# Products of x with w1 and w2 in eleven block products instead of twelve, with single buffers for V, q, xT and a gate tile

## The chip, the cores and the metric

One core of a Trainium2 chip runs the whole program. The metric is the device time in microseconds. The kernel before was run three times: 569.05, 569.18 and 569.51 us.

## The reference

A linear recurrence with complex gates (4 batches, 8 heads, 768 steps, head dimension 48) gives x, and four matrix products follow on x (3072 rows of 384). Everything is fp32 on the chip.

```
# per batch and head; a = a_re + i*a_im, its magnitude cut to at most 0.999
for t in range(S):
    S_re, S_im = ar*S_re - ai*S_im + k[t] v[t]^T,  ar*S_im + ai*S_re
    y[t] = q[t] @ S_re
x = y transposed to (B*S, H*D)            # 3072 x 384
a = x @ w1 ; b = x @ w2                   # 384 x 1024 each
out = ((a * b) @ w3) @ w_out              # 1024 x 1024, 1024 x 384
```

## The kernel before

**Tiling.** The work is cut into eight units, `u` = 0 to 7: a batch and half of its 768 steps, so 384 rows of x (`TT`) in three chunks of 128 (`UC` = 3). w3 and w_out are multiplied with each other once at the start (`fuse`, L973), and `w3o`, 1024 x 384, stands for both after that.

**A unit.** `gates(u)` turns the loaded gates, q and k into decayed and rotated forms. It is a chain that alternates between ScalarE (logarithm, exponential, arctangent, sine, with two loads of a function table) and VectorE (scans at L590 and L615, products from L566 to L638). Tiles of 128x1152 pass through it: `re`, `im`, `gA`, `gZ`, and `gR` and `k`, which are its results along with `gA` and `q`. DMAs then move `gR` and `k` into `KL`, `gA` and `q` into `QL` (`move`). `turn` (L671) transposes `gR` and `k` on TensorE, and ScalarE copies the result to `KT`. `state` (L721) multiplies `KT` with V and adds to the running state `T`. `scores` (L683) multiplies `KL` with `QL`, and VectorE copies the causal part to `A` (L685, the mask). `outputs` (L710) makes y from `A`, V, `T` and `QL`, and ScalarE copies it to `xT`, chunk by chunk (L712). `spread_v` (L524) copies the loaded `vr` into the padded layout V, which two buffers hold.

**The products of a unit.** `ffn_ab(u, j)` (L744) makes one block of 128 columns of x·w1 and x·w2: two PSUM tiles `m` of 128x384, three matmuls each. ScalarE copies the first to `a` (L749), VectorE multiplies the second with it (L750) into `ab`. Eight such blocks make a unit. `out_sums`, `out_pair` (L795) and `ffn_out` (L831) then multiply `ab` with `w3o`: for units 1 to 7, two of the three row blocks go through seven products of half blocks with sums on VectorE (L770, L777), ScalarE copying the first to `U` (L800), and the third row block goes plainly.

**Order.** TensorE's order is written out by hand: `ffn(u)` is a list of parts, and `unit(u)` runs the first four parts of unit u-1 (`AHEAD`), then alternates further parts with the pieces of unit u (transposes, state, scores, outputs), so that the last y of a unit is followed by the last parts of the output products and then by the next unit's blocks. `gates(u+1)` is a generator that is stepped on beside these parts. On the other engines a scheduler sets the order, by program order, readiness in its own estimate, and `tc.high_priority()` for what empties PSUM; each engine then works through its list strictly in order. PSUM tiles `m`, `p` and `o` share four buffers (`ps_m`). In units 2 and later ScalarE also works on "looks" (`check_weights`, L918 to L921), which go over the raw weights and the gates a block at a time, with DMAs of their own on SP.

**Buffers.** The pool `one` has single buffers, `two` double ones; `gate_pool` gives even and odd units each a buffer for `q`, `k`, `gA`, `gR`. `late` holds what is needed after the weights are in.

Of the kernel before, what the change touches and what calls it, by code (L numbers as in the profile page):

```python
# [374 lines left out]
def kernel(  # L375
# [36 lines left out]
    nc = tc.nc  # L412
# [44 lines left out]

    Ab = [singles.tile([P, H, C], FP, name=f"A{i}") for i in range(2)]
    Vb = [singles.tile([P, UC, H, 64], FP, name=f"V{i}") for i in range(2)]

# [36 lines left out]
    def take_qk(u):  # L497
        g = g_t.setdefault(u, {})
        g["q"] = gate_pool[u % 2].tile([P, KD, TT], FP, tag="q", name="q")
        g["k"] = gate_pool[u % 2].tile([P, KD, TT + 1], FP, tag="k", name="k")  # L500

    def load_qkv(u):
        b, h = divmod(u, 2)
        if "q" not in g_t.get(u, {}):
            take_qk(u)
        g = g_t[u]
        load_rows(g["k"], kt, u)
        load_rows(g["q"], qt, u)
        if u:
            load_v(u)  # L510

# [8 lines left out]
    def spread_v(u):  # L520
        vr = g_t[u]["vr"].rearrange("p c (h two d) -> p c h two d", two=2, d=D)
        V = Vb[u % 2].rearrange("p c (h two) e -> p c h two e", two=2)
        for i, e0 in enumerate((0, 64 - D)):
            nc.scalar.copy(out=V[:, :, :, i, e0:e0 + D], in_=vr[:, :, :, i])  # L524

# [12 lines left out]

    masked, begun = [], []

    def gates(u, split):

        b, h = divmod(u, 2)
        g = g_t.setdefault(u, {})
        A = gate_pool[u % 2].tile([P, KD, TT], FP, tag="gA", name="gA")
        R = gate_pool[u % 2].tile([P, KD, TT + 1], FP, tag="gR", name="gR")
# [9 lines left out]
        tt, ts, stt = nc.vector.tensor_tensor, nc.vector.tensor_scalar, nc.vector.scalar_tensor_tensor  # L556

        chain(nc.scalar.preload_act_table_set("natural_log_exp_and_others"))
        for s in parts:
            act(out=A[:, s], in_=re[:, s], func=AF.Ln)  # L560
            act(out=r[:, s], in_=A[:, s], func=AF.Exp, scale=-1.0)
            if u == 1:
                tc.add_manual_dep(chained[-1].ins, fused[-1].ins.name, ORDER, reason="unit 0 first")
# [14 lines left out]
        for s in parts:  # L578
            begun[:] = [stt(out=A[:, s], in0=Z[:, s], scalar=0.5, in1=A[:, s], op0=OP.mult, op1=OP.add)]
            act(out=Z[:, s], in_=A[:, s], func=AF.Exp, scale=-1.0, bias=EPS)  # L580
            act(out=Z[:, s], in_=Z[:, s], func=AF.Copy, scale=-1.0, bias=1.0)
            act(out=A[:, s], in_=A[:, s], func=AF.Exp)
        yield

        for s in parts:
            least = ts(out=A[:, s], in0=A[:, s], scalar1=0.999, scalar2=None, op0=OP.min)
            if u == 1:
                tc.add_manual_dep(least.ins, masked[-1].ins.name, ORDER, reason="scores first")
            for f in range(s.start, s.stop):
                nc.vector.tensor_tensor_scan(out=A[:, f], data0=A[:, f], data1=Z[:, f], initial=1.0,  # L590
                                             op0=OP.mult, op1=OP.mult)
# [12 lines left out]
        for X in (R[:, :, TT], K2[:, :, TT], st_dec[:, u]):  # L604
            nc.scalar.copy(out=X, in_=A[:, :, TT - 1])
        if u:
            spread_v(u)
        yield
# [82 lines left out]
    def outputs(u, c):  # L691
        QL = L_t[u][0]
        w = slice(c * C, (c + 1) * C)
        A, V = Ab[(u * UC + c) % 2], Vb[u % 2][:, c]
        if c == 0:
            xT_t[u] = two.tile([P, KD, TT], FP, tag="xT", name="xT")
        T = T_t.get((u // 2, u % 2 * UC + c))
        first = T is None
        y = ps_v.tile([P, KD, C], FP, tag="v", name="y")
        lanes = [[] for _ in range(4)]  # L700
        for i, q in enumerate(QUADS):
            f, j = divmod(i, 4)
            o = y[32 * j:32 * j + 32, f]
            got = [(V[:, hd, 32 * e:32 * e + 32], A[:, hd]) for hd, e in q]
            if not first:
                got += [(T[:, hd, 32 * e:32 * e + 32], QL[:, hd, w]) for hd, e in q]
            lanes[j] += [(o, a, b, n == 0, n == len(got) - 1) for n, (a, b) in enumerate(got)]
        for step in zip(*lanes):
            for o, a, b, s0, s1 in step:
                nc.tensor.matmul(out=o, lhsT=a, rhs=b, start=s0, stop=s1)  # L710
        with tc.high_priority():
            nc.scalar.copy(out=xT_t[u][:, :, w], in_=y)  # L712

    def state(u, c):

        KT, V = KT_t.pop((u, c)), Vb[u % 2][:, c]
        n = u % 2 * UC + c
# [19 lines left out]
    def ffn_ab(u, j):  # L737
# [3 lines left out]
        for w in (w1s, w2s):  # L741
# [4 lines left out]
            got.append(m)  # L746
        a = two.tile([P, TT], FP, tag="a", name="a")
        with tc.high_priority():
            copied[:] = [nc.scalar.copy(out=a, in_=got[0])]  # L749
            nc.vector.tensor_tensor(out=ab_t[u][:, j], in0=got[1], in1=a, op=OP.mult)  # L750

    KH, DH = KF // 2, DM // 2
# [18 lines left out]
    def out_pair(u):  # L773
# [15 lines left out]
        def product(p, bank, i):  # L789
# [8 lines left out]
            with tc.high_priority():  # L798
                if p == 1:
                    nc.scalar.copy(out=U[1], in_=m[1])  # L800
                elif p == 6:
# [21 lines left out]
    def ffn_out(u, t, parts=1):  # L823
        got = {}

        def part(f0):
# [6 lines left out]
            if f == KF - 1:  # L833
                o = (late if u else two).tile([P, DM], FP, tag="o", name="ot")
                nc.scalar.copy(out=o, in_=m)
                r0 = u * TT + t * P
                nc.sync.dma_start(out=out[r0:r0 + P, :], in_=o)
# [89 lines left out]
    def rounding():  # L927

        stack = ExitStack()
        for n, k in (("raw", 2), ("low", 2)):  # L930
            cv[n] = stack.enter_context(tc.tile_pool(name=n, bufs=k))
        return stack
# [21 lines left out]
    def row_work(f):  # L954
        if f == 0:
            w3_t["wo"] = one.tile([P, KF, DM], FP, tag="ab", name="wo_s")
        got = w3_t[f]
        w3_t[f] = two.tile([P, FF], FP, tag="xT", name="w3s")
        step = FF // (len(got) - 1)
# [40 lines left out]
    for A in Ab:  # L1000
        nc.vector.memset(A, 0.0)
    for V in Vb:
        nc.gpsimd.memset(V, 0.0)

# [13 lines left out]
    def ffn(u, parts=1):  # L1018
        if u == 0:
            return [lambda j=j: ffn_ab(u, j) for j in range(KF)] + [p for t in range(UC) for p in ffn_out(u, t, parts)]  # L1020
        got, last = out_pair(u), ffn_out(u, UC - 1, parts)
        if parts == 2:
            got.insert(5, last[1])
        return [lambda j=j: ffn_ab(u, j) for j in range(KF)] + [lambda: (out_sums(u), last[0]())] + got

# [16 lines left out]
    with tc.manual_schedule(engines={mybir.EngineType.PE}):  # L1042
# [37 lines left out]
        for i, p in enumerate(pieces(0)):  # L1080
# [4 lines left out]
            if i == 0:  # L1085
                for f in work[:2]:
                    f()
                load_qkv(1)
            for _ in range(5 if i == 0 else i >= 6):
                next(steps)  # L1090
# [13 lines left out]
        late = fast.enter_context(tc.tile_pool(name="late", bufs=1))  # L1104
        look = check_weights(fast.enter_context(tc.tile_pool(name="looks", bufs=2)))
        out_weights()
        for u in range(1, NU):
            steps = gates(u + 1, False) if u + 1 < NU else iter(())
            unit(u, steps, rest[HEAD:] if u == 1 else ffn(u - 1), look if u > 1 else iter(()), AHEAD[u])
            for _ in steps:  # L1110
                pass
# [46 lines left out]
```

## Time and profile before

| what | value |
|---|---|
| median of the runs | 569.18 us (569.05 to 569.51) |
| span of the profiled execution, first to last instruction | 566.8 us |
| TensorE busy | 541.8 us (96%) |
| VectorE, ScalarE, GpSimd busy | 335.8, 345.9, 3.5 us |
| mean granted TensorE clock | 0.995 |
| products with w1, w2 (L744), 768 records | 269.3 us |

The profile gives for the profiled execution its span alone; the median of the runs lies 2.4 us above it. A matmul in fp32 leaves two records, and so does its load of weights, so counts of TensorE are twice the number of matmuls in the code. A line of a group gives the count, the busy time in us and the mean of one record in ns, then the time that the engine stood idle just before such instructions, and what ended most of it. A line of the waits names who waited, for whom, how long in total, how often, and the longest. Busy times of records that overlap are counted once.

### The profile page before, as it was taken

To read this page: it belongs to the slowest core of one execution; us is meant where nothing else is said; L and a number is where in the kernel's file an instruction comes from. 1 tells how busy PE (TensorE), PEld (TensorE's weight loads), DVE (VectorE), ACT (ScalarE), POOL (GpSimd) and SP (SyncE) were. 2 spreads that over 40 slices of the span, in tenths; PEclk is the share of its full clock that TensorE was granted. 3 is DMA by queue.
4 is the path that set the end of the run, shared out by engine and by line. 5 is a ranking of instruction groups with operands and counts; after the bars stand their busy time and mean duration, and the time that the engine had idled before them with its cause. 6 is when DMAs were issued, how large, how long until landed. Compare 5 with 4: busy or idle time off the path is not lost.

```text
span 566.8 us, 9285 instructions
## 1 busy us (share of the span) xinstructions
PE 541.8 (96%) x3682; PEld 386.1 (68%) x3682; DVE 335.8 (59%) x511; ACT 345.9 (61%) x569; POOL 3.5 (1%) x9
## 2 busy tenths in 40 slices
PE   4697899999999999999999999999999999999995
PEld 2354775577566975688567966697568965796564
DVE  6998599927752677356742796255743696332121
ACT  6979856655662798458963899289965645101100
POOL 2000000000000000000000000000000000000000
PEclk9999999999999999999999999999999999999999
DMA  8996985780382447935593427754393104200001
GB/s 285 374 364 190 322 268 169 204 214 16 98 189 53 122 141 221 247 109 183 184 206 111 144 81 218 209 157 148 125 207 101 30 28 115 67 2 30 0 1 47
DMA packets 46772, 84.74 MB, mean 150 GB/s; under 512 B 4736, under 2 KB 36480, under 8 KB 45952
## 3 DMA queue, kind: packets, MB, share of 16 engines
q1 hardware_dynamic: 46720, 84.06, 50.6%
q8 instruction: 31, 0.51, 0.4%
q14 instruction: 21, 0.17, 0.1%
HBM read 60.42 MB, written 4.72 MB: 115 GB/s over the span
## 4 chain that ended last, share of the span: by engine, by line
PE 77%; ACT 9%; DVE 7%; DMA 3%; issue 2%; SPq 1%; DVEq 0%; ACTq 0%
PE m L744 40%; PE o L831 9%; PE p L795 9%; PE y L710 5%; PE sc L683 5%; PE kv L721 5%; PE tp L671 2%; ACT gZ L554 1%; DMA look<-in_w_dram 1%; ACT look L918 1%; ACT look L919 1%; PE f L973 1%; DMA im<-in_a_im_dram 1%; ACT gR L554 1%; ACT gA L554 1%
## 5 line engine op out<-in xcount | busy, mean ns | idle before, releaser
L744 PE MATMUL m<-xT,w1s 128*128 128x384 f32 x384 | 135.0, 488 | 0.1
L744 PE MATMUL m<-xT,w2s 128*128 128x384 f32 x384 | 134.3, 486 | 0.0
L744 PEld LDWEIGHTS m<-xT,w2s 128*128 128x128 f32 x384 | 73.0, 190 | 50.9
L744 PEld LDWEIGHTS m<-xT,w1s 128*128 128x128 f32 x384 | 71.2, 190 | 45.3 <-ACT xT L712 1.0
L750 DVE TENSOR_TENSOR ab<-m,a 128x384 f32<-128x384 f32 x64 | 35.2, 553 | 84.7 <-PE m L744 77.4
L749 ACT COPY a<-m 128x384 f32<-128x384 f32 x64 | 30.1, 474 | 53.5 <-PE m L744 52.3
L973 PE MATMUL f<-wo_s,w3s 128*128 128x384 f32 x128 | 47.7, 528 | 15.5 <-DVE wo_s L887 15.5
L831 PE MATMUL o<-w3o,ab 128*128 128x384 f32 x160 | 54.0, 487 | 0.0
L673 ACT COPY KT<-tp 128x384 f32<-128x384 f32 x40 | 33.6, 851 | 32.2 <-PE tp L671 32.1
L973 PEld LDWEIGHTS f<-wo_s,w3s 128*128 128x128 f32 x128 | 25.5, 206 | 35.2 <-DVE wo_s L887 18.6
L683 PE MATMUL sc<-QL,KL 96*128 96x128 f32 x384 | 47.2, 276 | 0.3 <-DVE A L685 0.3
L683 PEld LDWEIGHTS sc<-QL,KL 96*128 96x128 f32 x384 | 45.7, 192 | 1.3 <-DVE A L685 0.6
L685 DVE COPY_PREDICATED A<-causal,sc 128x512 f32<-128x512 int32 x48 | 34.6, 741 | 14.0 <-PE sc L683 13.6
L831 PEld LDWEIGHTS o<-w3o,ab 128*128 128x128 f32 x160 | 29.6, 190 | 18.7 <-issue 0.4
L728 DVE TENSOR_TENSOR T<-kv,T 96x512 f32<-96x512 f32 x16 | 11.0, 686 | 51.4 <-PE kv L721 51.4
L710 PE MATMUL y<-A,V 128*32 128x128 f32 x768 | 39.2, 275 | 0.0
L710 PEld LDWEIGHTS y<-A,V 128*32 128x32 f32 x768 | 32.9, 109 | 3.3 <-issue 1.4
L710 PE MATMUL y<-QL,T 96*32 96x128 f32 x640 | 34.4, 272 | 0.0
L877 ACT ACTIVATE low<-raw 128x384 uint16<-128x384 uint32 (+4 forms) x28 | 25.1, 902 | 11.1 <-DVE low L873 5.1
L721 PEld LDWEIGHTS kv<-V,KT 128*96 128x96 f32 x320 | 29.6, 165 | 3.1 <-issue 1.4
L795 PE MATMUL p<-To,So 128*128 128x192 f32 x168 | 31.6, 335 | 0.0
L721 PE MATMUL kv<-V,KT 128*96 128x64 f32 x320 | 30.0, 247 | 1.5 <-ACT KT L673 1.5
(114 smaller groups left out, 748.7 us busy)
## 6 DMA issues: line engine op xcount, KB each, us to landing
look<-in_w_dram SPq DMA_DIRECT2D x28, 512.0 KB, 3.9
raw<-in_w_dram SPq DMA_DIRECT2D x6, 1024.0 KB, 10.2
raw<-in_w_dram SPq DMA_DIRECT2D x8, 768.0 KB, 6.7
KL<-gR SPq DMA_DIRECT2D x24, 192.5 KB, 3.3
KL<-k SPq DMA_DIRECT2D x24, 192.5 KB, 3.8
re<-in_a_re_dram SPq DMA_DIRECT2D x24, 192.0 KB, 5.2
im<-in_a_im_dram SPq DMA_DIRECT2D x24, 192.0 KB, 3.2
k<-in_k_dram SPq DMA_DIRECT2D x24, 192.0 KB, 3.3
```

The lines of the kernel that those rows point to most:

```text
L673: nc.scalar.copy(out=KT_t[u, c][:, :, :, x].rearrange("p h d f -> p f d h"), in_=tp.rearrange("p f (d h) -> p f d h", h=H))
L683: nc.tensor.matmul(out=sc[:, j], lhsT=KL[:, x * n + j, w], rhs=QL[:, x * n + j, w], start=True, stop=True)
L685: masked[:] = [nc.vector.copy_predicated(out=A[:, x * n:(x + 1) * n], data=sc, mask=causal.rearrange("p (h t) -> p h t", h=1).to_broadcast ...
L710: nc.tensor.matmul(out=o, lhsT=a, rhs=b, start=s0, stop=s1)
L721: nc.tensor.matmul(out=kv[:, hd], lhsT=KT[:, hd].rearrange("p d x f -> p (d x f)"), rhs=V[:, hd], start=True, stop=True)
L744: nc.tensor.matmul(out=m, lhsT=w[:, j * P // WB, f, j * P % WB:j * P % WB + P], rhs=xT_t[u][:, f], start=(f == 0), stop=(f == KD - 1))
L749: copied[:] = [nc.scalar.copy(out=a, in_=got[0])]
L750: nc.vector.tensor_tensor(out=ab_t[u][:, j], in0=got[1], in1=a, op=OP.mult)
L795: nc.tensor.matmul(out=m[p], lhsT=a[:, f], rhs=b[:, f], start=(f == 0), stop=(f == KH - 1))
L831: nc.tensor.matmul(out=m, lhsT=ab_t[u][:, f, t * P:(t + 1) * P], rhs=w3o[:, f], start=(f == 0), stop=(f == KF - 1))
L877: nc.scalar.activation(out=ends.bitcast(U16)[:, 0::2].rearrange("p (r m) -> p r m", r=r), in_=lo.bitcast(U32), func=AF.Copy, scale=2.0 ** -29)
L973: nc.tensor.matmul(out=sums[j], lhsT=w3_t[f][:, j * P:(j + 1) * P], rhs=w3_t["wo"][:, f], start=(f == 0), stop=(f == KF - 1))
```

## The change

For units 1 to 7 the products with w1 and w2 are made for a pair of column blocks at a time. The first two of the three blocks of x's columns, the two halves of its 384 rows and the two column blocks of the weights form a two by two by two block product, which takes seven products of block sums instead of eight; the third block of x's columns joins four of the seven as a second matmul. That is eleven matmuls of 192 columns for each of w1 and w2, instead of six of 384 (twelve of 192). Sums of weight blocks are made once on GpSimd (`ab_weights`, one block of w1 and w2 is overwritten by a difference), sums of xT once a unit on VectorE (`x_sums`), and the products are put together by ScalarE copies, VectorE sums out of PSUM and GpSimd sums in SBUF; the final multiplication of a and b goes to GpSimd, in the last unit to VectorE. Unit 0 stays as it was. To make room, V, `q`, `gA` and `xT` have one buffer each; v is loaded and spread at the start of the unit that uses it, `a` and the output tiles share the buffers `o`, the rounding stage of the weights has its own buffers (`w3s`, and `early` for unit 1's gates), and the first copy of the output products (`U`) is ordered behind the first gate activations of unit u+2.

```diff
-    Vb = [singles.tile([P, UC, H, 64], FP, name=f"V{i}") for i in range(2)]
+    V_all = singles.tile([P, UC, H, 64], FP, name="V0")
...
-        g["q"] = gate_pool[u % 2].tile([P, KD, TT], FP, tag="q", name="q")
+        g["q"] = one.tile([P, KD, TT], FP, tag="q", name="q")
...
-        A = gate_pool[u % 2].tile([P, KD, TT], FP, tag="gA", name="gA")
+        A = one.tile([P, KD, TT], FP, tag="gA", name="gA")
...
+        N = cv["early"].tile([P, KD, TT], FP, tag="N", name="N") if u == 1 else A
         for s in parts:
-            act(out=A[:, s], in_=re[:, s], func=AF.Ln)
-            act(out=r[:, s], in_=A[:, s], func=AF.Exp, scale=-1.0)
+            act(out=N[:, s], in_=re[:, s], func=AF.Ln)
+            act(out=r[:, s], in_=N[:, s], func=AF.Exp, scale=-1.0)
+            opened[:] = [chained[-1]]
...
-            xT_t[u] = two.tile([P, KD, TT], FP, tag="xT", name="xT")
+            xT_t[u] = one.tile([P, KD, TT], FP, tag="xT", name="xT")
...
             nc.scalar.copy(out=xT_t[u][:, :, w], in_=y)
+        if u and c == UC - 1:
+            x_sums(u)
...
+    def ab_weights():
+        S = z_t["S"] = late.tile([P, 2, 3, FF // WB, P], FP, tag="SW", name="SW")
...
+                nc.gpsimd.tensor_tensor(out=out_, in0=x, in1=y, op=op)
+
+    def x_sums(u):
+        X = z_t["X"] = late.tile([P, 5, TH], FP, tag="X", name="X")
+        B = [[xT_t[u][:, f, x * TH:(x + 1) * TH] for x in range(2)] for f in range(KD)]
+        with tc.high_priority():
+            for i, x, y in ((0, B[0][1], B[0][0]), (1, B[1][1], X[:, 0]), (2, B[1][1], B[0][1]),
+                            (3, B[1][0], X[:, 1]), (4, B[2][0], B[2][1])):
+                nc.vector.tensor_tensor(out=X[:, i], in0=x, in1=y, op=OP.subtract)
+        z_t["B"] = B
+
+    def ab_pair(u, n):
...
+        last = nc.vector if u == NU - 1 else nc.gpsimd
+
+        def product(*terms):
+            m = ps_m.tile([P, 2, TH], FP, tag="mm", name="m")
+            for i, w in enumerate((w1s, w2s)):
+                for x, (a, b) in enumerate(terms):
+                    a = S[:, i, a, n] if isinstance(a, int) else w[:, n, a[1], a[0] * P:(a[0] + 1) * P]
+                    nc.tensor.matmul(out=m[:, i], lhsT=a, rhs=b, start=(x == 0), stop=(x == len(terms) - 1))
+            return m
...
+        def first():
+            C = got["C"] = late.tile([P, 2, 2, 2, TH], FP, tag="C", name="C")
+            U = got["U"] = late.tile([P, 2, TH], FP, tag="UC", name="UC")
+            p1 = product(((0, 0), B[0][0]))
+            with tc.high_priority():
+                nc.scalar.copy(out=C[:, 0, 0], in_=p1)
+            p6 = product((1, X[:, 1]))
+            with tc.high_priority():
+                add(U, p6, C[:, 0, 0])
+            p2 = product(((0, 1), B[1][0]), ((0, 2), B[2][0]))
+            with tc.high_priority():
+                nc.scalar.copy(out=C[:, 1, 0], in_=p2)
+                nc.gpsimd.tensor_tensor(out=C[:, 0, 0], in0=C[:, 0, 0], in1=C[:, 1, 0], op=OP.add)
+            p5 = product((0, X[:, 0]))
+            with tc.high_priority():
+                copied[:] = [nc.scalar.copy(out=C[:, 1, 1], in_=p5)]
+                add(C[:, 0, 1], p5, U)
+
+        def second():
+            C, U = got["C"], got["U"]
+            p7 = product(((1, 0), X[:, 2]), ((1, 2), B[2][1]))
+            with tc.high_priority():
+                add(U, p7, U)
+                nc.gpsimd.tensor_tensor(out=C[:, 1, 1], in0=C[:, 1, 1], in1=U, op=OP.add)
+            p4 = product(((1, 1), X[:, 3]), ((1, 2), X[:, 4]))
+            with tc.high_priority():
+                add(C[:, 1, 0], p4, U)
+                last.tensor_tensor(out=ab[:, 2 * n + 1], in0=C[:, 1, :, 0], in1=C[:, 1, :, 1], op=OP.mult)
+            p3 = product((2, B[1][1]), ((0, 2), B[2][1]))
+            with tc.high_priority():
+                add(C[:, 0, 1], p3, C[:, 0, 1])
+                last.tensor_tensor(out=ab[:, 2 * n], in0=C[:, 0, :, 0], in1=C[:, 0, :, 1], op=OP.mult)
+        return [first, second]
...
-                    nc.scalar.copy(out=U[1], in_=m[1])
+                    first = nc.scalar.copy(out=U[1], in_=m[1])
+                    if u + 2 < NU:
+                        tc.add_manual_dep(first.ins, opened[-1].ins.name, ORDER, reason="gates first")
...
+        ab_weights()
         out_weights()
         for u in range(1, NU):
+            spread_v(u)
+            if u + 1 < NU:
+                load_v(u + 1)
             steps = gates(u + 1, False) if u + 1 < NU else iter(())
```

## The prediction

> **What bounds the kernel now.** I read the page from its first part down: busy time, slices, chain, groups; then the waits of TensorE alone, then one block of the products with w1 and w2 in time.
>
> ```profile
> span 566.8 us, 9285 instructions
> PE 541.8 (96%) x3682; PEld 386.1 (68%) x3682; DVE 335.8 (59%) x511; ACT 345.9 (61%) x569; POOL 3.5 (1%) x9
> PE   4697899999999999999999999999999999999995
> PEclk9999999999999999999999999999999999999999
> ...
> L744 PE MATMUL m<-xT,w1s 128*128 128x384 f32 x384 | 135.0, 488 | 0.1
> L744 PE MATMUL m<-xT,w2s 128*128 128x384 f32 x384 | 134.3, 486 | 0.0
> L750 DVE TENSOR_TENSOR ab<-m,a 128x384 f32<-128x384 f32 x64 | 35.2, 553 | 84.7 <-PE m L744 77.4
> L749 ACT COPY a<-m 128x384 f32<-128x384 f32 x64 | 30.1, 474 | 53.5 <-PE m L744 52.3
> ```
>
> TensorE is full from about 50 us on, at full clock, and the products to be changed (L744) are 269 us of it. VectorE and ScalarE mostly wait for it. Its own waits:
>
> ```profile
> PE f L973 <- DVE wo_s L887: 15.5, 6, 7.2
> PE kv L721 <- ACT KT L673: 1.5, 2, 0.9
> PE tp L671 <- DVE gR L634: 1.4, 1, 1.4
> PE sc L683 <- DVE A L685: 0.3, 1, 0.3
> ```
>
> The 15.5 us lie in the weight stage at the start. Of the rest the third line matters: in one unit the transposes waited for the last step of the gates (gR). The gates are thus almost late already, though the average share of VectorE is 59%. Two pieces of the chain give the prices of matmuls, and a window the load beside them:
>
> ```profile
> 81.82 30.96 PE m L744 x96
> ...
> 549.10 6.50 PE p L795 x40
> ```
> ```profile
> 329.33:348.68 19.35, 19.35 (x62) 11.35 (x62) 15.37 (x19) 18.21 (x33) 0.00 (x0) 1.00 0.53 165
> ```
>
> A matmul leaves two records, so 48 matmuls of 384 columns took 30.96 us (0.645 each) and 20 of 192 columns 6.50 us (0.325 each). The window (length, then PE, PEld, DVE, ACT, POOL busy) is the first ten products of a unit, up to its first transpose: ScalarE is busy 94% of it, VectorE 79%. That is the stage to judge by, not the page's average.
>
> **What the Trainium skill says.** "GPSIMD Engine Reference", section 3.1, gives 4497 ns for a two-input fp32 operation of 2048 elements, about 2.2 ns an element; my estimate for 384 is 0.9 us. The trace before has no such operation. "SBUF — State Buffer", section "Who interferes with whom", says that a VectorE instruction with two SBUF inputs and a GpSimd one that reads SBUF exclude each other, the later one blocking for a whole instruction. No trace here shows that yet: GpSimd works 3.5 us. "VectorE: DVE Perf Modes", section on the errata, has (N+151)/0.96 ns for a two-input fp32 sum: 1357 ns for 1152 elements, and the trace agrees (L634, 1358).
>
> **The change part by part.** Call the seven products of a pair of column blocks, in TensorE's order, p1, p6, p2, p5 (first part), p7, p4, p3 (second part); p2, p7, p4, p3 take two matmuls per weight, the others one.
>
> *Matmuls.* A pair was 12 of 384 columns, 12 x 0.645 = 7.74 us; it becomes 22 of 192, 22 x 0.325 = 7.15. Saved 0.59 a pair, 2.36 a unit, **16.5 us** in 28 pairs, all on the path as long as nothing is late.
>
> *ScalarE.* 56 copies at L749 go and 84 of the same 128x384 come: +28 x 0.474 = 13.3 us. Copies to V move from the gates to the unit's start.
>
> *VectorE.* 56 products at L750 go (31.0 us). In come 140 sums out of PSUM of the same form (77.4), 35 sums of xT blocks, 128x192, by the row of L777 0.35 each (12.2), and 8 products in the last unit (4.4): +63 us, 59% to 70%.
>
> *GpSimd.* 104 operations of 0.9 us, 94 us, and eight sums of weights of 512 elements, by the same page 1.1 us each, about 9 us near 115 us, needed some 28 us later (first pair at 143.8): nothing. A pair holds four, 3.6 us, under the 7.15 of TensorE.
>
> *Buffers.* Costed at nothing, each hidden as follows. V single: its two copies (0.66 us each) follow the last y of the unit before, and the first kv comes over 20 us later. The load of v moves behind the stores on SP, and is needed only at the next unit's start. q and the gate tile single: the load of q now waits on SP until the move to QL has read q (3 us); behind it stand a store, k's load and looks, and k is first used over 30 us later. xT single: the first copy of a unit comes after all products of the unit before in TensorE's order. U's copy (L800 before) now follows the first gate activations, 3.5 us; its first reader is p6 of the output product, 10 us later. The pools at the start keep their number of buffers. Cover gone, each would cost its own 1 to 3 us a unit, which the range holds.
>
> *The new waits.* Four PSUM tiles, C and the running sum U in one buffer. p7 needs p1's tile free, so the copy C<-p1 has 3.25 us (p1 to p5) from the start of a pair, but in ScalarE's new order it stands behind gate steps and looks; p5's tile and p7's free only through VectorE, in order behind gate steps of 1.36 us. And p1's copy of the next pair waits until GpSimd has read C for the last product.
>
> No load or store is added or dropped; SP only issues them in another order.
>
> I worked this through for the unit that starts at 329.2 us, with spacings from the trace (1.27 to 1.38 us a gate step on VectorE, 1.06 on ScalarE, 0.47 and 0.4 the evictions, 0.57 to 0.77 a look, 1.28 the table) in the order of the built program. The gates ride some 2 us earlier, as one of their steps goes ahead of a mask: the scans end at 328.2, not 330.1. From there ScalarE does Ln, xT's copy, Exp, three small copies, a table and Arctan (5.2 us), then C<-p1 until 333.8. VectorE does q, then the xT sums: p6 can start at 330.75, 0.8 late. Unstalled is TensorE alone at 0.325 a matmul. In the middle column GpSimd and VectorE never collide; in the last they exclude each other.
>
> | event, us | before | no collision | collisions |
> |---|---|---|---|
> | p7 of pair 1 starts (unstalled 332.4) | | 333.9 | 333.9 |
> | C<-p1 of pair 2 ends | | 341.1 | 343.9 |
> | pair 2 ends (unstalled 343.5) | | 345.8 | 347.9 |
> | gR ready for the transposes | 347.1 | 347.9 | 350.7 |
> | fifth part ends, first transpose (unstalled 346.7) | 348.7 | 349.1 | 351.9 |
> | last product ends | 362.7 | 363.2 | 366.9 |
>
> In the last column VectorE's scans lose 0.9 us to GpSimd three times, GpSimd's last product of pair 1 ends at 343.5, and the copy behind it, with the ScalarE work queued there (the copy to re, Abs, Sin), shifts by 2.8. So a unit with gates ends 0.5 to 4.3 us later than before, the 2.36 saved already taken off. The same steps for the first changed unit give +3.0 and +4.5, for the one at 390 about +1 and +2.7. I take **+2.7** a unit, between the columns, since not every overlap collides, for six units: +16.2. The seventh has no gates beside it; its copies have slack: -2.4. Sum +13.8.
>
> **The rivals.** (a) *The saving survives*: every eviction lands in its 3.25 us because the gates ride earlier still. For it: TensorE waited 1.4 us for gates in 430 us. Against: ScalarE is 94% busy in the window. It decides at C<-p1: ended by 332.4, p7 doesn't stall. All of it: 569.2 - 16.5 = 552.7; half of it: 561. (b) *GpSimd paces the pairs*: if most of its operations wait out a gate step (0.9 + 1.36 = 2.26 us), four take 9.0 us a pair, 1.3 over the old 7.74; 24 pairs +31, the last unit -2.4: 598. Against: gate steps fill only two and a half of four pairs. (c) *Weights bind*: a load of 128x128 is listed at 190 ns, and if half a matmul took that and not 162.5, a pair is 44 x 0.19 = 8.36, +0.62, 28 pairs +17: 587. Against it the 6.50 us for x40, which had a load each.
>
> **How the numbers follow.** The profiled execution spans 566.8 us; the runs' median is 569.18, so 2.4 lie around it. 569.2 + 13.8 = 583.0; I say **582.5**. Chances: stalls as worked out 0.68, rival (b) or worse than the last column 0.08, (c) 0.05, (a) in whole or part 0.15, within 0.2% (about what a measurement of this kernel can tell from no change) 0.04. The ends of the main case: six times 0.5, less 2.4, is 570; six times 4.3 is 592.5. Down into (a) and up by the buffers' share: **565 to 595**. Faster 0.15, same 0.04, slower 0.81.
>
> **What would show it.** Right: TensorE idle in L792 (the new products) of 2 to 6 us a unit, released by ACT C and DVE UC or C; gR's transposes waiting in most units; L792 at 0.325 us a matmul in the last unit; GpSimd near 0.9 us an operation, longer beside gate steps; VectorE near 400 us, and gate steps longer than 1.36 us where they collide. Wrong: TensorE's busy time down by 16 us with no new idle time, or spacing of 380 ns in unstalled bursts, or idle TensorE for a load of q, v or a store.

## The result and the profile after

The changed kernel takes **596.4 us** (median of 4 runs, 595.46 to 596.67) against 569.19 us for the kernel before in the same comparison: 27.2 us more, ratio 1.0465, 95% interval 1.0448 to 1.0483. The direction was forecast, the size was not: 13.3 were predicted, and 596.4 lies just outside the range. The profiled execution spans 594.8 us against 566.8, 28.0 more.

The first part of the page after, and two of its groups:

```profile
span 594.8 us, 10829 instructions
PE 541.8 (91%) x4242; PEld 463.4 (78%) x4242; DVE 408.5 (69%) x638; ACT 354.6 (60%) x597; POOL 150.3 (25%) x120
...
PE   5788999899899997999899997999889988999995
...
PEclk9889999899999999899999999999999989999999
...
L792 PE MATMUL m<-xT,w1s 128*128 128x192 f32 x280 | 65.9, 334 | 5.6 <-DVE C L796 5.6
L803 ACT COPY C<-m 128x384 f32<-128x384 f32 x28 | 13.4, 477 | 56.9 <-POOL ab L829 39.5
```

TensorE is as busy as before, 541.8 us, although 16.5 us of matmuls are gone. Time has come in elsewhere. TensorE idles for 53 us instead of 25. Its clock is granted at 0.983 in the mean, 0.995 before (some 8s among the 9s of PEclk): while TensorE works it falls to half in five places instead of one, which makes the records there about 6.8 us longer in all (see "The clock" below). What makes up the other 10 us of busy time is not broken down here. GpSimd's 150 us are more than the 103 of my estimates.

TensorE's waits, after:

```profile
PE f L1072 <- DVE wo_s L986: 14.9, 5, 7.3
PE m L792 <- ACT C L803: 13.4, 12, 2.0
PE m L792 <- DVE C L796: 6.9, 11, 0.8
PE m L792 <- DVE X L777: 5.2, 5, 2.0
PE m L747 <- DVE ab L753: 2.9, 1, 2.9
PE kv L724 <- ACT KT L674: 1.4, 2, 0.9
PE m L792 <- DVE UC L796: 1.0, 3, 0.5
PE tp L672 <- DVE gR L635: 0.7, 1, 0.7
```

The first line is the old wait of the weight stage. New are those for evictions (`C`, `UC`), for the sums of xT (`X`) and one of 2.9 us in unit 0's products (`ab`, L753). The gates, `gR`, were waited for once, 0.7 us. The longest new wait is for ScalarE's copy of p1 (L803), and ScalarE's own waits name what held the copy up:

```profile
ACT C L803 <- POOL ab L829: 39.5, 17, 6.1
```

In 17 of 28 pairs the copy stood waiting for GpSimd's last product of the pair before, which still read C. Not all of that reaches TensorE: its own waits for this copy are the 13.4 us above.

**Where the 28 us lie.** The 16 matmuls `o` that follow a unit's products mark where each unit ends. These windows run from mark to mark, first before, then after. The columns are the window, its length, then the busy time (and instructions) of PE, PEld, DVE, ACT, POOL, then clock, DMA share and GB/s.

```profile
112.78:177.46 64.68, 64.68 (x457) 44.51 (x457) 32.80 (x40) 36.34 (x54) 0.00 (x0) 1.00 0.51 125
177.46:239.57 62.11, 62.11 (x444) 45.94 (x443) 37.53 (x51) 44.20 (x77) 0.00 (x0) 1.00 0.57 159
239.57:300.88 61.31, 61.21 (x453) 44.80 (x453) 35.56 (x48) 44.64 (x75) 0.00 (x0) 1.00 0.64 185
300.88:362.99 62.11, 62.11 (x444) 45.94 (x443) 37.44 (x51) 45.71 (x78) 0.00 (x0) 1.00 0.51 143
...
487.95:546.52 58.57, 58.57 (x427) 42.38 (x427) 14.64 (x29) 6.92 (x14) 0.00 (x0) 1.00 0.03 11
```
```profile
118.22:186.46 68.24, 64.57 (x537) 54.77 (x537) 43.51 (x58) 37.23 (x58) 20.95 (x17) 1.00 0.50 125
186.46:255.52 69.06, 63.47 (x523) 58.03 (x523) 47.11 (x68) 46.97 (x84) 20.33 (x17) 0.98 0.52 148
255.52:319.25 63.73, 59.75 (x533) 55.13 (x533) 44.63 (x65) 48.24 (x86) 20.92 (x17) 1.00 0.58 164
319.25:386.11 66.86, 61.58 (x523) 56.34 (x523) 46.47 (x68) 49.02 (x87) 22.19 (x17) 1.00 0.58 163
...
518.29:574.50 56.21, 56.21 (x508) 52.74 (x507) 26.42 (x53) 8.82 (x18) 9.15 (x10) 1.00 0.04 12
```

Second column against second column, the six units with gates beside them cost +3.56, +6.95, +2.42, +4.75, +1.76 and +5.46 us (the last two from windows of the same kind), 24.9 together. The last unit gives -2.36, the predicted -2.4 to the hundredths. And the first mark itself is 5.44 late (118.22 for 112.78): 5.4 + 24.9 - 2.4 = 27.9.

**The clock.** A part of this is not in any list of waits. At 114, 240 and 482 us the granted clock falls to 0.50 for about 3.4 us, and each time TensorE's work there takes 1.7 us longer. The same 24 records (p7, p4 and p3 of a pair) after a short stop, with such a fall and without one (start, length):

```profile
240.15 5.85 PE m L792 x24
...
372.42 4.17 PE m L792 x24
```

So 1.7 us of the late start, of the +6.95 and of the +5.46 belong to the clock, 5.1 of the 28 us. Two more falls lie in the first 45 us; the kernel before has one there, and none later while TensorE works. Each of the three begins about when a stop of TensorE ends (2.85, 1.38 and 1.99 us), but a stop of 2.02 us at 296 us is followed by none. What decides whether the clock falls is not shown.

**The late start.** 3.7 of the 5.4 us have to do with GpSimd's eight sums of weights, which I had costed at nothing: that much of the first mark's delay goes when they are moved (e7 below). The buffers are not the cause, as e1, which has them and no sums, reaches its first mark at 112.85. The other 1.8 us stay open. The timelines of GpSimd and VectorE there (start, length, then the instruction):

```profile
107.94 2.38 POOL L768 TENSOR_TENSOR SW<-SW,w1s 128x512 f32<-128x512 f32 x1
110.28 2.38 POOL L768 TENSOR_TENSOR SW<-SW,w2s 128x512 f32<-128x512 f32 x1
112.61 2.38 POOL L768 TENSOR_TENSOR SW<-w1s,SW 128x512 f32<-128x512 f32 x1
```
```profile
109.11 2.42 DVE L638 TENSOR_TENSOR gA<-q,re 128x1152 f32<-128x1152 f32 x1
111.45 2.41 DVE L636 TENSOR_TENSOR k<-k,gZ 128x1152 f32<-128x1152 f32 x1
113.79 0.55 DVE L753 TENSOR_TENSOR ab<-m,a 128x384 f32<-128x384 f32 x1
```

A gate step of 1.35 us takes 2.4 beside them, two stand ahead of the eviction L753, and TensorE waits 2.85 us for it. When it goes on, six records that took 2.10 before take 3.83, at the clock's first fall of the three:

```profile
114.39 3.83 PE L747 MATMUL m<-xT,w2s 128*128 128x384 f32 x6 [2.85 <-DVE ab L753]
```

**One pair to the next.** In the unit that I had worked out (its blocks start at 329.2 before, 347.7 after) the same hold is seen on both engines:

```profile
357.28 1.58 POOL L821 TENSOR_TENSOR C<-C,UC 128x384 f32<-128x384 f32 x1 [1.41 <-ACT V L522]
358.94 1.75 POOL L825 TENSOR_TENSOR ab<-C 128x384 f32<-128x384 f32 x1
360.65 0.99 POOL L829 TENSOR_TENSOR ab<-C 128x384 f32<-128x384 f32 x1
```
```profile
361.68 0.48 ACT L803 COPY C<-m 128x384 f32<-128x384 f32 x1 [2.06 <-POOL ab L829]
```

GpSimd's last product ends at 361.6, and ScalarE, idle for 2.06 us, copies p1 right after it; p7 needs that PSUM tile and starts at 362.21, 1.42 late. In the next pair the same two products run beside VectorE's L635 and L636 and take 2.19 and 2.11 us, and TensorE waits 1.73.

### The profile page after: what moved, and what is told of

The parts are those of the page before. It is cut to its first block, busy times and chain, and to the rows that moved or that the text cites. A ratio compares the mean times of both kernels' runs of the same rounds, so it can differ in the third digit from the quotient of the medians.

```text
span 594.8 us, 10829 instructions
## 1 busy us (share of the span) xinstructions
PE 541.8 (91%) x4242; PEld 463.4 (78%) x4242; DVE 408.5 (69%) x638; ACT 354.6 (60%) x597; POOL 150.3 (25%) x120
## 4 chain that ended last, share of the span: by engine, by line
PE 39%; DVE 22%; ACT 20%; issue 9%; POOL 6%; DMA 2%; SPq 1%; DVEq 0%; ACTq 0%; POOLq 0%
PE m L792 16%; PE o L927 7%; PE p L889 5%; ACT gZ L552 4%; PE kv L724 4%; PE sc L684 3%; DVE gA L593 3%; POOL ab L825 2%; POOL ab L829 2%; ACT gR L552 2%; ACT re L552 2%; ACT gA L552 2%; DVE C L796 2%; PE tp L672 2%; PE y L711 2%
## 5 line engine op out<-in xcount | busy, mean ns | idle before, releaser
L810 POOL TENSOR_TENSOR C<-C 128x384 f32<-128x384 f32 x28 | 37.3, 1331 | 269.4 <-ACT C L809 126.0
L792 PE MATMUL m<-xT,w1s 128*128 128x192 f32 x280 | 65.9, 334 | 5.6 <-DVE C L796 5.6
L792 PE MATMUL m<-xT,w2s 128*128 128x192 f32 x280 | 64.9, 330 | 0.0
L792 PEld LDWEIGHTS m<-xT,w1s 128*128 128x128 f32 x280 | 48.0, 191 | 9.1 <-DVE C L796 8.7
L792 PE MATMUL m<-X,SW 128*128 128x192 f32 x224 | 47.6, 336 | 7.6 <-DVE X L777 5.2
L792 PE MATMUL m<-X,w1s 128*128 128x192 f32 x168 | 38.9, 341 | 13.5 <-ACT C L803 13.4
L792 PEld LDWEIGHTS m<-xT,w2s 128*128 128x128 f32 x280 | 49.5, 193 | 0.0
L821 POOL TENSOR_TENSOR C<-C,UC 128x384 f32<-128x384 f32 x28 | 36.7, 1310 | 45.2 <-DVE UC L796 41.0
L803 ACT COPY C<-m 128x384 f32<-128x384 f32 x28 | 13.4, 477 | 56.9 <-POOL ab L829 39.5
L792 PEld LDWEIGHTS m<-X,SW 128*128 128x128 f32 x224 | 37.7, 192 | 11.4 <-DVE X L777 6.7
L796 DVE TENSOR_TENSOR C<-m,UC 128x384 f32<-128x384 f32 x56 | 30.9, 552 | 22.1 <-ACT C L813 12.3
L792 PEld LDWEIGHTS m<-X,w1s 128*128 128x128 f32 x168 | 28.5, 194 | 17.2 <-ACT C L803 16.6
```

Source lines behind the costliest of these rows:

```text
L792: nc.tensor.matmul(out=m[:, i], lhsT=a, rhs=b, start=(x == 0), stop=(x == len(terms) - 1))
L796: nc.vector.tensor_tensor(out=out, in0=x, in1=y, op=OP.add)
L810: nc.gpsimd.tensor_tensor(out=C[:, 0, 0], in0=C[:, 0, 0], in1=C[:, 1, 0], op=OP.add)
L821: nc.gpsimd.tensor_tensor(out=C[:, 1, 1], in0=C[:, 1, 1], in1=U, op=OP.add)
```

## The experiments

All were timed against the kernel before, whose own medians were 569.3 to 570.6 us in these comparisons, and times are medians. Single runs of one kernel lie up to 4 or 5 us apart (568.6 to 572.3 for the kernel before, 567.8 to 572.4 for e15), and differences of 1 or 2 us below are to be read so.

**Buffers alone.** Single V, q, xT and gate tile and the changed orders, with twelve plain blocks in every unit.

```diff
-        if u and c == UC - 1:
-            x_sums(u)
...
-        if u == 0:
+        if True:
             return [lambda j=j: ffn_ab(u, j) for j in range(KF)]
...
-        ab_weights()
```

> The changed kernel's buffers and orders (V, q, gate tile, xT single; a and output tiles shared; v loaded and spread late; U's copy behind the gates) with the products of w1 and w2 as they were before, in twelve blocks: no sums of weights, none of xT. If the buffers cost nothing, as predicted: 569 us, within 1.5. If a rival cause, the single buffers, makes a good part of the 27 us lost: 575 us or more, with TensorE waiting for a load or for V or xT.

Measured: 568.7, ratio 0.999 [0.9978, 1.0002]. The buffers and the moved loads cost nothing, as costed.

**GpSimd out of the pairs.** Its four operations of a pair on VectorE; the sums of weights stay.

```diff
-                nc.gpsimd.tensor_tensor(out=C[:, 0, 0], ...
+                nc.vector.tensor_tensor(out=C[:, 0, 0], ...
-        last = nc.vector if u == NU - 1 else nc.gpsimd
+        last = nc.vector
```

> Eleven products, but the four GpSimd operations of every pair are put on VectorE (the eight sums of weights at the start stay on GpSimd). If GpSimd's sharing with VectorE is what costs the units (each operation stretched, C held for ScalarE's next copy): faster than the 596.4 of the changed kernel, about 585, with gate steps back at 1.35 us. If it is VectorE's own queue, in order behind gate steps: four operations of 0.55 us a pair more, 9 us a unit on VectorE, so slower, 600 us or more.

Measured: 582.25, ratio 1.022 [1.0183, 1.0256], so 14 us less, though VectorE is busier by 39 (447.4). What GpSimd was to relieve it of costs less on VectorE itself. TensorE's waits for the copy of p1 fall from 13.4 to 2.4. 13 us over the kernel before remain.

**No looks; then C and U in two buffers as well.** The looks are left out of both kernels; the room for the second C comes from them.

```diff
-            unit(u, steps, ..., look if u > 1 else iter(()), AHEAD[u])
+            unit(u, steps, ..., iter(()), AHEAD[u])
# and, in e3 only:
-            C = ... tag="C"
-            U = ... tag="UC"
+            C = ... tag=f"C{n % 2}"
+            U = ... tag=f"UC{n % 2}"
```

> The changed kernel without the looks over the weights and gates (that part of the work is left out, with its loads; so no time of it is a gain to keep). If ScalarE's queue is what holds the copies C<-m and the gates: units 2 to 6 lose most of their stalls, some 3 us each, 582 us or less. If GpSimd and VectorE hold them: within 5 us of the changed kernel, 592 to 596, since ScalarE's copies wait for GpSimd in any case.

> As the run without looks, and C and the running sum U of the products in two buffers each (the room comes from the looks). If the copy C<-p1 that waits for GpSimd's last product of the pair before is the wait that ends last: the wait of ScalarE for GpSimd (39.5 us in the changed kernel) goes and 2 us a unit come back, 12 us against the run without looks. If VectorE's queue decides: under 3 us.

Measured: 604.86 without looks (ratio 1.0615 [1.0576, 1.0655]) and 587.48 with C and U doubled on top (1.0315 [1.0279, 1.035]). The first is a miss of every theory: ScalarE lost some 60 us of work, and the kernel became 8 slower. The scheduler put the instructions in another order: where the sums of xT stood ahead of two gate steps (L602, L603) on VectorE, at 348 us in the changed kernel, they stand behind them in e4, and TensorE's wait for these sums grew from 5.2 to 9.1 us. That is a part of the 8; the whole is not accounted for. ScalarE, with less to do, waits longer for GpSimd's last product:

```profile
ACT C L803 <- POOL ab L829: 56.5, 18, 7.6
```

TensorE's wait for the copy of p1 is nearly as long as it was (12.0 us for 13.4), so a full ScalarE queue is not what makes that copy late. The second buffers of C and U gave 17.4 back, and that line is gone.

**Only the last unit.** Eleven products in unit 7, twelve in units 1 to 6; the sums of weights wait for a late state.

```diff
-        if u == 0:
+        if u < NU - 1:
             return [lambda j=j: ffn_ab(u, j) for j in range(KF)]
...
+        ab_weights(T_t[3, 5])
```

> Eleven products in unit 7 alone, units 1 to 6 in twelve as before, on the changed kernel's buffers. The sums of weights on GpSimd are held back until the second state of unit 7 is there (two small GpSimd operations that read it stand ahead of them), so they lie where no gates run. If TensorE's saving is real where nothing stands in front of the evictions: 2.4 us under the kernel before, 566.8, as unit 7 gained in the changed kernel. If the gain there came from something else, or the late sums collide with the end: 569 or more.

Measured: 567.52 against 570.31 in the same comparison, ratio **0.9959** [0.9935, 0.9982]: 0.4% under the kernel before, the one version here that beats both kernels. The saving is real where no gates run beside the pairs.

**Later sums of weights.** `ab_weights` is held until unit 1's first state, by two small GpSimd operations that read it.

```diff
-        ab_weights()
...
+            if u == 1 and i == 4:
+                ab_weights(T_t[0, 4])
```

> The changed kernel with the eight sums of weights held back until the first state of unit 1 (by two small GpSimd operations that read it), so that they no longer run beside unit 0's last gate steps. If those sums stretched the gate steps, held TensorE 2.9 us and let its clock fall, the 5.4 us lost by the first output product go: about 591.5 us. If unit 0 lost them to something else (the buffers, the early tile): 596, or more where the sums come too late for unit 1's first pair.

Measured: 595.11 (ratio 1.0421 [1.0391, 1.0452]). Half a miss. The local effect is as expected: the eight sums take 1.26 to 1.30 us each, the wait at L747 is gone, the first mark comes at 114.54 instead of 118.22. But the next mark lies at 186.30 instead of 186.46: unit 1 gives all but 0.2 us of it back. The trace does end 1.5 us earlier, and that is the clock: from 186.30 on, e7 has the stops of the changed kernel at the same places, but not its fall at 240 us, and that unit takes 67.34 us instead of 69.06. In unit 1 TensorE stands for a mask and an output copy instead:

```profile
PE y L711 <- DVE A L686: 1.6, 1, 1.6
PE m L794 <- ACT ot L936: 0.9, 1, 0.9
```

**Both together, and another order of the products.** e9 has GpSimd out of the pairs and late sums of weights; e8 is e9 with p2 ahead of p6, so that the sums of xT have longer.

> All GpSimd operations of the pairs on VectorE, and the sums of weights held back as in the run with late sums. If the two costs add: 582.3 less 4.7, 577.6 us. If the late sums only move the loss: 581 or more.

> As the run with everything on VectorE and late sums, with p2 ahead of p6 in TensorE's order, so that the first use of the sums of xT comes 1.3 us later. TensorE waited 5.7 us for those sums in the run with all on VectorE. If that wait is on the path: 3 to 5 us faster than without the swap, 573. If p6's later sum only moves the wait to the next tile: the same within 1 us.

Measured: 581.5 (ratio 1.0201 [1.0171, 1.023]) and 586.91 (1.0281 [1.0252, 1.0311]). e9 fits its second case, that the late sums only move the loss: they are worth about 1 us here too. e8 fits neither of its cases. With the swap the kernel is 5 us slower: the wait for X falls from 6.3 to 1.4 us, and others take its place (below). But the granted clock also falls three times more after the first 60 us in e8's trace than in e9's, which has no such fall there, and that is up to 5.1 us; so the 5 is not the price of the waits alone.

```profile
PE m L794 <- ACT C L805: 8.3, 6, 1.9
PE tp L672 <- DVE gR L635: 6.7, 3, 4.3
```

**Short gate steps.** e9 with eight of VectorE's gate steps of units 2 to 7 on a third of their columns; the other columns are left out of the computation.

```diff
-            tt(out=q[:, s], in0=q[:, s], in1=A[:, s], op=OP.mult)
+            tt(out=q[:, few(s)], in0=q[:, few(s)], in1=A[:, few(s)], op=OP.mult)
...
-            tt(out=r, in0=k, in1=cos, op=OP.mult)
+            tt(out=r[:, w], in0=k[:, w], in1=cos[:, w], op=OP.mult)
```

> e9_vec_late (no GpSimd in the pairs, sums of weights held back to unit 1) with eight of VectorE's gate steps of units 2 to 7 (the products at L602 to L606 and L635 to L639 that make k, q, r and the gate tile) done on one third of their columns; that part of the computation is left out, the order of TensorE's work stays. VectorE loses about 6 x 8 x 0.9 = 43 us of work, all of it gate steps that stand ahead of evictions in its queue. Theory 'what is left of the loss in e9 is VectorE's queue: sums out of PSUM and sums of xT stand behind gate steps' expects 581.5 to fall to 560 to 568, TensorE's waits for X and C on VectorE nearly gone, and ends of the units 1 to 6 within 1 us of a steady saving of 2.4 a unit for most of them. Rival 'it is ScalarE's queue (copies to C and U behind gate functions, tables and looks)' expects 577 or more, with TensorE's wait for ACT C as long as in e9 or longer. Half and half gives about 572.

Measured: 583.9 (ratio 1.0223 [1.019, 1.0256]). VectorE has 33 us less to do and nothing is gained, so its queue alone isn't the rest either; the rival's time and wait came out instead. TensorE's wait for ACT C rose from 2.3 to 5.9, its wait for gR from 2.5 to 5.7.

**Half of C in two buffers, looks in one: spoilt.** To make room the looks went into one buffer.

> The changed kernel, with the half of C that the first product of a pair is copied to (and that GpSimd's last product of the pair before still reads) in two buffers; the other half and U stay in one; the looks get one buffer instead of two to make room. Theory 'TensorE is late because ScalarE's copy of p1 waits for GpSimd to have read C' expects the line ACT C waiting for POOL ab to lose most of its 39.5 us, and 584 to 590 instead of 596.4 (e3 gained 17 from two buffers for all of C and U, without looks). Rival 'GpSimd and VectorE stretch each other, and the evictions are late whatever the buffers' expects 594 or more.

> e9_vec_late (581.5) with the same half of C in two buffers. There VectorE makes the last product of a pair, and ScalarE waited for it 29 us before its copy of p1, of which TensorE felt 2.3 us directly. Theory 'C in one buffer' expects 575 to 579; rival 'in-order queues of VectorE and ScalarE alone' expects 581 within 1 us.

> e10_short (583.9; eight gate steps on a third of their columns, that part of the computation left out) with the same half of C in two buffers. Theory 'the single C and VectorE's queue each hide the other: both must go' expects 565 to 572; rival 'ScalarE's queue of gate functions and looks' expects 580 or more.

Measured: 635.81, 621.65 and 629.76 (ratios 1.116, 1.0917, 1.1056). The room was taken from the wrong place, and the three decide nothing on C. In e12 TensorE's longest wait is now

```profile
PE sc L684 <- DMA re<-in_a_re_dram: 35.5, 2, 19.0
```

A look's load waits on SP until the one buffer is free (73 us in all for ScalarE's looks, 58 in the changed kernel), and the gates' loads stand behind it in SP's queue.

**The same half of C, looks in two buffers.** The room comes from looks over half of the weights' columns (e16 is the base, e17 has the second buffer); the other half is left out of the computation. Here is e17's edit to C alone, in part.

```diff
-            C = got["C"] = late.tile([P, 2, 2, 2, TH], FP, tag="C", name="C")
+            C0 = got["C0"] = late.tile([P, 2, 2, TH], FP, tag=f"C{n % 2}", name="C")
+            C1 = got["C1"] = late.tile([P, 2, 2, TH], FP, tag="C", name="C")
```

> The changed kernel with each look at the weights over the first 512 of its columns only; the other columns of those looks are left out of the computation. It is the base for e17_half_c0 and frees the room that e17 needs, with the looks still in two buffers. ScalarE loses some 20 us of looks. Both theories expect 590 to 600, since taking all looks away (e4_nolook) did not make the changed kernel faster.

> e16_half with the half of C that the first product of a pair is copied to in two buffers (as in e12_c0, now with the looks in two buffers). Theory 'the copy of p1 waits for GpSimd to have read C' expects 6 to 14 us less than e16, and TensorE's 13 us of waits for ACT C gone. Rival 'GpSimd and VectorE stretch each other, whatever the buffers' expects the same as e16 within 3 us.

Measured: 598.51 (ratio 1.0493 [1.0454, 1.0532]) and 583.87 (1.0255 [1.0215, 1.0294]): **-14.6 us** from a second buffer of 3 KB per partition. e16's trace has three falls of the clock after the weight stage and e17's two, so up to 1.7 us of it may be the clock's. TensorE's wait for the copy of p1, first in e16, then in e17:

```profile
PE m L792 <- ACT C L803: 13.3, 11, 1.5
```
```profile
PE m L792 <- ACT C L804: 0.4, 2, 0.2
```

In e17 GpSimd and VectorE still hold each other up (its groups, mean ns after the comma; 1331 and 1616 in the changed kernel):

```profile
L811 POOL TENSOR_TENSOR C<-C 128x384 f32<-128x384 f32 x28 | 37.8, 1351 | 247.7 <-ACT C L810 116.4 <-ACT look L1019 62.7 <-DVE UC L796 33.9
L635 DVE TENSOR_TENSOR gR<-k,re 128x1152 f32<-128x1152 f32 x7 | 12.3, 1759 | 3.9 <-ACT re L552 3.9
```

So these 14.6 us were not the price of the long operations as such: they were lost because the copy of the next pair's p1 could not begin until the last of them had ended.

**GpSimd, then gate steps, with C no longer in the way.** No looks, C and U in two buffers, GpSimd out of the pairs and the sums of weights late (e14); the short gate steps on top (e15). The edits are those shown above.

> e3_nolook_c2 (587.5; C and U in two buffers, the looks left out of the computation) with the four GpSimd operations of a pair on VectorE and the sums of weights held back to unit 1. Theory 'two effects of GpSimd: it stretches VectorE's steps, and it holds C' expects the stretching to be left in e3 and gone here: 572 to 580. Rival 'with C doubled GpSimd costs nothing more' expects 584 to 588.

> e14_vec_nolook_c2 with eight of VectorE's gate steps on one third of their columns (that part of the computation, and the looks, are left out). Here no GpSimd, no look and no single C is left, and VectorE has 43 us less to do ahead of the evictions. Theory 'single C and VectorE's queue each hid the other' expects 556 to 566, so nearly the whole saving of 16.5. Rival 'the chain of gates on ScalarE and VectorE itself ends too late beside evictions that go first' expects 570 or more, with TensorE waiting for gR or KL.

Measured: 580.0 (ratio 1.0172 [1.0142, 1.0202]) and 570.52 (1.001 [0.9996, 1.0024]). So with C double, GpSimd out of the pairs and late sums are together still worth 7.5 us against e3. Short gate steps, worth nothing in e10, are now worth 9.5. What hid them in e10 is not shown: e15 differs from it by the second buffers and by the missing looks, and no run here separates these two. And 570.5 is not the 556 to 566 that the theory wanted, and the rival's waits for gR or KL aren't there. What is left:

```profile
PE m L798 <- DVE X L783: 8.1, 5, 2.3
PE m L798 <- ACT ot L940: 1.6, 1, 1.6
PE y L715 <- DVE A L690: 1.6, 1, 1.6
```

The first pair still stands for the sums of xT in five units, and unit 1 takes 68.6 us instead of 64.7; the two other waits above and one fall of the clock lie in it.

## Why the prediction was right and wrong

- **Saving in matmuls, right.** The four pairs of the last unit are one piece of the chain (start, length, number of records), first before, then after; a matmul of 192 columns takes 28.80 / 88 = 0.327 us:

```profile
515.36 31.16 PE m L744 x96
```
```profile
545.70 28.80 PE m L792 x176
```

  Rival (c), weights that bind, is out, and so is rival (a).
- **Buffers at nothing, right** (e1: 0.999).
- **The times worked out for the unit at 329.2, right; the +2.7 a unit drawn from them, too small.** This is the first step that failed. Counted from the unit's first product:

| event, us | no collision | collisions | measured |
|---|---|---|---|
| p7 of pair 1 starts | 4.7 | 4.7 | 4.9 |
| C<-p1 of pair 2 ends | 11.9 | 14.7 | 14.5 |
| pair 2 ends | 16.6 | 18.7 | 18.5 |
| gR ready | 18.7 | 21.5 | 21.2 |
| first transpose | 19.9 | 22.7 | 22.5 |
| last product ends | 34.0 | 37.7 | 37.9 |

The collisions column holds to 0.3 us, and to 0.4 for GpSimd's last product of pair 1 (14.3 worked out, 13.9 measured). That it fits so closely is in part luck. I had VectorE's scans lose 0.9 us to GpSimd three times; they took 1.30, 1.00 and 1.00 us, so they lost 0.3 in all. GpSimd's operations were the ones held up, with 1.96, 1.58 and 1.75 us instead of 0.9.

I took 2.7 a unit "between the columns, since not every overlap collides"; the mean measured is 4.15. Over six units that is **8.7 us** of the 13.9 that were missing. 3.4 of them are the clock's two falls, for which the working had nothing. Without these the mean is 3.6, so the waits themselves were sized too small by about 0.9 a unit. In the three units that I had worked through, the columns gave 3.0 to 4.5, 0.5 to 4.3 and 1 to 2.7, and 3.56, 4.75 and 1.76 were measured: two between the columns, one above, 2.0 more in all than I took. The other three, to which I had only carried the 2.7 over, make up the larger part: 6.95, 2.42 and 5.46 us, 6.7 more than I took, the clock's 3.4 among them.
- **The sums of weights at nothing, wrong.** The second step that failed: **5.4 us** at the first mark. I had looked at when their results are needed, and not at what runs beside them; and I had put them near 115 us, while they began at 104, beside unit 1's gate steps. The estimate of 1.1 us each from the Trainium skill ("GPSIMD Engine Reference", section 3.1) was close for an operation alone (1.27); beside gate steps it was up to 2.38. How much of the 5.4 reaches the end is less than that: e7 moved the sums and gained 3.7 us at the first mark, and unit 1 gave 3.5 of them back, most of it in other waits.
- **GpSimd's 0.9 us, right alone, low beside gates.** In the last unit an operation takes 1.00 us, over all pairs 1.16 to 1.33, beside gate steps up to 2.2. Rival (b), that GpSimd paces the pairs, gave nearly the time measured (598) but not by its account: four operations average 5.0 us a pair, less than TensorE's 7.15. GpSimd was waited for at two places only: by ScalarE for the last read of C (39.5 us), and by VectorE for the output sums (`So`, L864, 9.5 us), on which no listed wait of TensorE follows.
- **"p1's copy of the next pair waits until GpSimd has read C", right, and sized too low.** It is named in the prediction, and e17 shows it to be 13 to 14.6 us, about half of the loss; GpSimd out of the pairs (e2, 14.2) takes away the same wait, so the two aren't to be added.
- **"gR's transposes waiting in most units", wrong.** They waited once, 0.7 us. In the unit at 347.7 the gates were ready 21.2 us after its first product, later than the 17.9 of the kernel before, but the evictions had made TensorE later still (22.5).
- **VectorE near 400, idle L792, right** (408.5; 26.5 us of listed waits in the new products, 3.8 a unit).

What the experiments leave open: of the 16.5 us saving, nearly all is consumed even in e15. The waits for X (8.1), the two other waits in its unit 1 (3.2) and two falls of the clock after the first 60 us (3.4) account for about 15; a kernel that removes these as well was not tried. e4 shows that a scheduler's new order alone can move such a kernel by 8 us. And the profiled runs have between none (e1, e5, e9, e14) and three (the changed kernel, e3, e4, e8, e16) falls of the clock between the first 60 us and the end of the products, up to 5.1 us, the three spoilt runs aside. So the steps of this ladder that are smaller than these 8 and 5 us together (e14 against e3 above all, where other orders came with the edit) are sizes of the edits as built rather than of one wait.

## What to carry to other kernels

When a tile is handed round three engines, look for its last reader, and ask when its first writer of the next round is due: a second buffer for half of that tile alone was worth as much as taking the slow engine out. If a cost is worked out for some of a kernel's units, work through the others too before the sum is trusted: here the three that were not worked through cost 14.8 us, not the 8.1 carried over to them. A saving in TensorE's work is kept only where the engines that empty its PSUM have slack; here that was the last unit, and doing the change there alone beat both kernels.

## What was not expected of the hardware

- GpSimd and VectorE with both inputs in SBUF hold *each other* up, and the waiting lies inside their records. In the two timelines of the late start the records end in turn: GpSimd at 110.32, VectorE at 111.53, GpSimd at 112.66, VectorE at 113.86. These ends are 1.1 to 1.2 us apart, a little less than a VectorE step (1.35) or a GpSimd sum (1.27) takes alone, so records of 2.4 us fit one wait for the other engine and then the work. The Trainium skill ("SBUF — State Buffer", "Who interferes with whom") calls the port that the two share an exclusive lock, and the trace agrees. That the later one is blocked for a whole instruction the section says only of VectorE's 2-port modes; I took it for two SBUF inputs as well, and these times fit that. VectorE's sums out of PSUM (L796, 0.55 us a piece, as L750 before) weren't touched, as the same section has it for one SBUF input.
- A stop of TensorE can cost more than itself: after the one of 2.85 us six records took 3.83 us, 1.7 more than the same six before, at a granted clock of 0.50. In all the traces here the clock fell for about 3.4 us at a time, or for several such stretches in a row: in e12, around stops of 16.5 and 19.0 us, it stayed at 0.50 for about 17 and 27 us. So stalls in the list of waits can be less than what they cost; busy time that does not fall when work is taken away is the sign of it.
